# Gated linear attention and a mixture of experts: state read in four array tiles, another order of loads, filler matmuls

## The chip, the cores and the metric

One NeuronCore of a Trainium2 chip runs the whole kernel. The metric is device time in microseconds (us) for one execution: lower is better. The kernel before takes 489.4 us, the median of three runs (488.76 to 489.51). The profile is of one more execution, whose span from first to last instruction is 488.0 us.

## The reference, cut to what matters

Two layers follow one another. The first is a recurrent attention with a decay per channel. The second sends each row to the one expert that its gate prefers.

```python
# q, k, v, alpha: batch 4, heads 8, sequence 768, head size 48, float32
for t in range(S):
    state = alpha[:, :, t, :, None] * state + np.einsum('bhd,bhe->bhde', k[:, :, t], v[:, :, t])
    y[:, :, t] = np.einsum('bhd,bhde->bhe', q[:, :, t], state)
# x: the heads side by side, 3072 rows of 384
x = np.ascontiguousarray(y.transpose(0, 2, 1, 3)).reshape(B * S, H * D)
# experts: 8 of them, w1 384 x 1024, w2 1024 x 384
expert_idx = np.argmax(x @ w_gate, axis=1)
# for the rows of each expert e:
h = np.maximum(rows @ w1[e], 0.0)
out_rows = gate_weight * (h @ w2[e])
```

## The kernel before: the parts that matter here

The sequence is cut into 24 blocks of 128 rows, six to each batch entry. Within a block the recurrence becomes matrix products. Its running product of decays is the exponential of a running sum of logarithms. What earlier blocks left behind is a state `U`, read once per block. Heads go two by two: head `a` of a pair lies on partitions `64a` to `64a + 47`.

```python
def load(s, names):                      # 1024 runs of 192 bytes each
    for n in names:
        ...
        nc.sync.dma_start(t[:], src)
def cums(s):                             # running sum of ln(alpha), then two exponentials
    cum = ps.tile([C, Dm], F32, name="cum")
    nc.tensor.matmul(cum[:], lhsT=cmask[:], rhs=d["ln"][:], start=True, stop=True)
    ...
def attend(s):
    y = ps.tile([C, NP, C], F32, name="y")
    if c > 0:                            # the state read: NP = 4 pairs, two heads each
        for p in range(NP):
            for r in (0, DP):            # DP = 64
                nc.tensor.matmul(y[r : r + DP, p, :], lhsT=st[s - 1]["U"][r : r + D, p, :],
                                 rhs=d["qT"][r : r + D, p, :], start=(p == 0), stop=False, ...)
    for p in range(NP):                  # the block's own values
        for i, r in enumerate((0, DP)):
            nc.tensor.matmul(y[r : r + DP, p, :], lhsT=d["v"][:, 2 * p + i, :],
                             rhs=d["d" + "AB"[i]][:, p, :], start=(c == 0 and p == 0), stop=True, ...)
    kvp = ps.tile([C, NP * D + 4 * E], F32, name="kvp")   # what the block adds to the state, and ranks
    ...                                  # matmuls into kvp
    nc.vector.tensor_copy(d["yT"][:], y[:])
    ...                                  # the new U, on VectorE and GpSimd
```

`rows(s)` turns `yT` back into rows with the constant `back`, whose last columns also hold the gate's weights. `keep_rows(s)` stores them to DRAM (`x_rows`). `choose` picks the expert of each row, `rank_products` and `slots_of` work out its place among the expert's rows, `one_hots` and `tokens_of_slots` collect in one PSUM bank which token is in which place, and `indices` makes of it the list for the gathers.

```python
for s in range(-5, NT + 1):              # NT = 24
    do(load, s + 8 if s + 8 >= 4 else -1, "akq")
    do(load, s + 5, "v")
    do(logs, s + 5)
    do(cums, s + 4)
    do(operands, s + 3)
    do(transposes, s + 2)
    ...                                  # at s == NT: tokens of places, ranks, one-hots
    do(rows, s - 1)
    do(scores, s + 1)
    do(keep_rows, s - 1)
    ...
    do(attend, s)
    ...
    if s == 15:
        w_t[0] = fetch1(0), fetch2(0)    # all of expert 0's weights: two transfers
...
indices(range(NX, NX + NJ))              # three parts of one tile, g_idx
indices(range(NX))
indices(range(NX + NJ, PB))
```

The experts come in four pairs. Each pair gathers seven blocks of 128 rows, turns them, and goes through two layers. Nothing holds back the weights of experts 1 and 2: they are issued as soon as the queue gets to them.

```python
xg = gather(columns(0))
w_t[1] = fetch1(1), fetch2(1)
w_t[2] = fetch1(2), fetch2(2)
for p in range(EP):
    ...
    if p == 0:
        for j in range(2):
            turn(xg, j, ...)
        for f, hp in enumerate(begun):   # three tiles of hidden units on the first 256 rows
            products1(w_t[0][0], xTa, hp, f, 0, 2 * C)
        turn(xg, 2, ...)
        turn(xg, NH, ...)
    ha = layer1(...)
    for j in range(NH + 1, NJ):
        turn(xg, j, ...)
    ...
```

Of the kernel before, what the change touches and what calls it, by code (L numbers as in the profile page):

```python
# [18 lines left out]
def kernel(  # L19
# [10 lines left out]
):  # L30

# [42 lines left out]

    consts = ctx.enter_context(tc.tile_pool(name="consts", bufs=1))
# [7 lines left out]

    def first_consts():
        make_upper_triangular(nc, cmask[:], 1.0, diag=True)
        make_identity(nc, ident[:])
        for t in kqb:
            nc.vector.memset(t[:, :, :, D:], 0.0)
        for t in vb:
            nc.vector.memset(t[:, :, D:], 0.0)  # L90
        for t in Ub + Eb:
            nc.vector.memset(t[:], 0.0)

        for a in range(2):
            r = slice(a * DP, a * DP + D)
            nc.vector.tensor_copy(
                back[r, :, a * D : (a + 1) * D], ident[r, None, a * DP : a * DP + D].to_broadcast([D, NP, D]),
            )
            nc.vector.tensor_scalar_mul(back[r, :, D2:], back[r, :, D2:], -1.0)
# [57 lines left out]
    oh_c = rte.tile([C, NT, NC], F16)  # L157
    g_idx = rte.tile([C, NC], I32)
    tot = rte.tile([C, E], F32)

# [4 lines left out]
    def fetch1(ex):  # L165
        w1 = wpool.tile([C, DB, F], F32, name="w1")
        nc.sync.dma_start(w1[:], moe_w1[bass.ds(ex, 1)].rearrange("e (a p) f -> p (e a) f", p=C))
        return w1

# [4 lines left out]


    with tc.tile_pool(name="ld", bufs=6) as ld, \
         tc.tile_pool(name="work", bufs=2) as work, \
         tc.tile_pool(name="ps", bufs=1, space=PSUM) as ps, \
         tc.manual_schedule():
# [6 lines left out]
        def load(s, names):  # L186
            for n in names:
                src = rows_of({"a": alpha, "k": k, "q": q, "v": v}[n], s)
                if n == "v":
                    st[s][n] = vb[s % len(vb)]  # L190
                    nc.sync.dma_start(st[s][n][:, :, :D], src)
                else:
                    t = ld.tile([C, H, D], F32, name=n + "_sb", bufs=4 if n == "a" else 6)
                    nc.sync.dma_start(t[:], src)  # L194
                    st[s][n] = t
# [70 lines left out]
        def attend(s):  # L266
# [3 lines left out]
            y = ps.tile([C, NP, C], F32, name="y")  # L270
            if c > 0:
                for p in range(NP):
                    for r in (0, DP):
                        nc.tensor.matmul(  # L274
                            y[r : r + DP, p, :], lhsT=st[s - 1]["U"][r : r + D, p, :], rhs=d["qT"][r : r + D, p, :],
                            start=(p == 0), stop=False, skip_group_check=True,
                        )
            for p in range(NP):
                for i, r in enumerate((0, DP)):
                    nc.tensor.matmul(  # L280
                        y[r : r + DP, p, :], lhsT=d["v"][:, 2 * p + i, :], rhs=d["d" + "AB"[i]][:, p, :],
                        start=(c == 0 and p == 0), stop=True, skip_group_check=True,
                    )
            d["yT"] = work.tile([C, NP, C], F32, name="yT")
            kvp = ps.tile([C, NP * D + 4 * E], F32, name="kvp")
            kv = kvp[:, : NP * D].rearrange("r (p d) -> r p d", p=NP)
            ranked = [rank_products(g, kvp[:, NP * D : NP * D + len(g) * E]) for g in groups_of if g[-1] == s - 2]
            if c + 1 < NB:
                for p in range(NP):
                    for i, r in enumerate((0, DP)):  # L290
                        nc.tensor.matmul(  # L291
                            kv[r : r + DP, p, :], lhsT=kqb[s % 4][:, 0, 2 * p + i, :], rhs=d["v"][:, 2 * p + i, :D],
                            start=(p == 0), stop=True, skip_group_check=True,
                        )
            nc.vector.tensor_copy(d["yT"][:], y[:])  # L295
# [88 lines left out]
        def indices(blocks):  # L384
# [3 lines left out]
            gv = g_idx[:].rearrange("p (a b) -> p a b", a=EP)[:, :, blocks[0] : blocks[-1] + 1]  # L388
# [7 lines left out]

        nc.scalar.preload_act_table_set("natural_log_exp_and_others")
        for i in range(2):
            load(i, "akq")
        nc.gpsimd.memset(back[:], 0.0)  # L400
        for a in range(2):
            nc.scalar.dma_start(
                back[a * DP : a * DP + D, :, D2:], moe_w_gate.rearrange("(p a d) e -> a d p e", a=2, d=D)[a],
            )
        for i in range(2, 4):
            load(i, "akq")
        first_consts()
        hots = []
        for s in range(-5, NT + 1):
            do(load, s + 8 if s + 8 >= 4 else -1, "akq")  # L410
            do(load, s + 5, "v")
            do(logs, s + 5)
            do(cums, s + 4)
            do(operands, s + 3)
            do(transposes, s + 2)
            if s == NT:
                route = ps.tile([C, Dm], F32, name="cum")
                tokens_of_slots(0, 6)
                ranked = rank_products(groups_of[-2], ps.tile([C, NP * D + 4 * E], F32, name="kvp")[:, :E])
                while hots:  # L420
                    one_hots(hots.pop(0))
                slots_of(*ranked)
                one_hots(hots.pop(0))
# [8 lines left out]
            do(attend, s)  # L432
            for _ in range(2 if len(hots) > 2 else 1):
                if hots and s < NT:
                    one_hots(hots.pop(0))
            late_consts(s)
            if s == 15:
                w_t[0] = fetch1(0), fetch2(0)
        tokens_of_slots(6, NT - 1)
        slots_of(*rank_products(groups_of[-1], ps.tile([C, NP * D + 4 * E], F32, name="kvp")[:, :E]))  # L440
# [5 lines left out]
        indices(range(NX, NX + NJ))  # L446
        indices(range(NX))
        indices(range(NX + NJ, PB))
# [4 lines left out]
    xg_pool = ctx.enter_context(tc.tile_pool(name="moe_x", bufs=2))  # L453
# [41 lines left out]
    def gather(idx):  # L495

        xg = xg_pool.tile([C, len(idx), W], F32, name="xg")
# [70 lines left out]
    def columns(p):  # L568
        c0 = p * PB + NX
        return [g_idx[:, c0 + j : c0 + j + 1] for j in range(NJ)]  # L570
# [3 lines left out]
    with tc.manual_schedule():  # L574
        xg = gather(columns(0))
        w_t[1] = fetch1(1), fetch2(1)
        w_t[2] = fetch1(2), fetch2(2)
        for p in range(EP):
            idx = columns(p)
            a, b = 2 * p, 2 * p + 1  # L580
            xg_next = gather(columns(p + 1)) if p + 1 < EP else None
            if p == 0:

                xTa = wk.tile([C, DB, CAP], F32, name="xT", bufs=3)
                xTb = wk.tile([C, DB, CAP], F32, name="xT", bufs=3)
                for j in range(2):
                    turn(xg, j, (xTa, j * C, 0, C))
                begun = [hidden_tile() for _ in range(3)]
                for f, hp in enumerate(begun):
                    products1(w_t[0][0], xTa, hp, f, 0, 2 * C)  # L590
                turn(xg, 2, (xTa, 2 * C, 0, C))
                turn(xg, NH, (xTa, NH * C, 0, HB), (xTb, 0, HB, C))
            ha = layer1(w_t[a][0], xTa, CAP, begun, 2 * C)
            begun = ()
            for j in range(NH + 1, NJ):
                turn(xg, j, (xTb, HB + (j - NH - 1) * C, 0, C))
            gw = gates(xg, NJ)
            w1n = {e: fetch1(e) for e in (a + 3,) if e < E}
            for j in range(NH):
                layer2([(w_t[a][1], ha, j * C)], gw[:, j : j + 1], idx[j], True)  # L600
            hb = layer1(w_t[b][0], xTb, CAP)
            if b + 3 < E:
                w1n[b + 3] = fetch1(b + 3)
            if xg_next is not None:
                xTa = wk.tile([C, DB, CAP], F32, name="xT", bufs=3)
                xTc = wk.tile([C, DB, CAP], F32, name="xT", bufs=3)
                for j in range(NH):
                    turn(xg_next, j, (xTa, j * C, 0, C))
                turn(xg_next, NH, (xTa, NH * C, 0, HB), (xTc, 0, HB, C))
                xTb = xTc  # L610
            if p == 0:
                extra_blocks()
            layer2([(w_t[a][1], ha, NH * C), (w_t[b][1], hb, 0)], gw[:, NH : NH + 1], idx[NH], True)
            if a + 3 < E:
                w_t[a + 3] = w1n[a + 3], fetch2(a + 3)
            for j in range(NH + 1, NJ):
                layer2([(w_t[b][1], hb, HB + (j - NH - 1) * C)], gw[:, j : j + 1], idx[j], True)
            if b + 3 < E:
                w_t[b + 3] = w1n[b + 3], fetch2(b + 3)
# [44 lines left out]
```

## Time and profile before

| | before |
|---|---|
| median of three runs | 489.4 us |
| span of the profiled execution | 488.0 us |
| TensorE busy (matmul) | 457.6 us, 94% of the span |
| VectorE, ScalarE, GpSimd busy | 142.3, 103.2, 137.8 us |
| mean granted clock of TensorE | 0.979 |
| bytes moved by DMA | 59.76 MB, 127213 packets, 110304 of them under 512 bytes |

The page of a profile gives busy time per engine, then the span in 40 slices with a digit for each (9 is 90% or more busy). It goes on with transfers, the chain of work that ended last, and the costliest groups of instructions. A line such as `L274 PE MATMUL y<-qT,Ub` names the kernel's line, the engine, the operation, the tile written and the tiles read. A matmul on 32-bit floats leaves two records: the 160 matmuls of the state read (eight in each of 20 blocks) are 320 records; a transpose leaves one. The records of neighbouring matmuls overlap, so a busy TensorE is not one at its peak, and the distance from start to start tells the pace.

### The profile page before, as it was taken

Reading aid. Unit: us, or ns where it says so; the run is one execution under the profiler, and the core shown is the slowest. Engines: PE = TensorE matmul, PEld = TensorE weight load, DVE = VectorE, ACT = ScalarE, POOL = GpSimd, SP = SyncE. Lnnn points to the kernel's source line nnn. Section 1 sums busy time; section 2 is a strip of 40 time slices with the busy share of each in tenths; the row PEclk is TensorE's granted clock in tenths of the full one; section 3 lists DMA queues with packets and bytes.
Section 4 is the critical chain, followed back from the end, with each engine's and each line's share of the span. In section 5 each row is a group of like instructions: output and inputs, shape, how many; then the busy total and the mean of one; then the engine's idle time right before and its main releaser. Section 6 shows DMA issues by size and latency. Waiting matters only on the chain.

```text
span 488.0 us, 7370 instructions
## 1 busy us (share of the span) xinstructions
PE 457.6 (94%) x2881; PEld 297.4 (61%) x2881; DVE 142.3 (29%) x391; ACT 103.2 (21%) x209; POOL 137.8 (28%) x226
## 2 busy tenths in 40 slices
PE   2999999999999389999999999999999999999992
PEld 0788888888898275555555555555555455555451
DVE  2344766665778421212401201101201201301100
ACT  3544544544421001101001111011111001101010
POOL 3556745555642270010124010016020020010020
PEclk9999999999999779999999999999999999999997
DMA  9999999889992151300726400537300040000000
GB/s 161 199 177 203 207 210 203 168 170 272 299 356 107 50 160 39 142 32 8 267 75 211 135 32 0 189 118 249 129 28 16 1 166 22 1 20 16 2 32 25
DMA packets 127213, 59.76 MB, mean 122 GB/s; under 512 B 110304, under 2 KB 121604, under 8 KB 127178
## 3 DMA queue, kind: packets, MB, share of 16 engines
q1 hardware_dynamic: 114818, 48.87, 39.6%
q0 software_dynamic: 3584, 10.34, 6.4%
q10 hardware_dynamic: 8776, 0.08, 1.0%
q8 instruction: 23, 0.38, 0.3%
q14 instruction: 12, 0.10, 0.1%
HBM read 49.70 MB, written 10.35 MB: 123 GB/s over the span
## 4 chain that ended last, share of the span: by engine, by line
issue 54%; PE 27%; POOL 11%; DVE 2%; DMA 2%; SPq 1%; ACT 0%; POOLq 0%; ACTq 0%
POOL out_dram L559 6%; POOL xg L499 5%; PE sA L254 5%; PE y L280 4%; PE tp L241 4%; PE xr L313 4%; PE cum L210 4%; PE y L274 4%; PE kvp L291 2%; SPq L194 1%; DMA a_sb<-in_alpha_dram 1%; DMA x_rows<-xs 1%; DVE yT L295 1%; DVE sc L330 0%; DVE dA L258 0%
## 5 line engine op out<-in xcount | busy, mean ns | idle before, releaser
L528 PE MATMUL hp<-xT,w 128*128 128x448 f32 (+2 forms) x402 | 148.4, 530 | 1.2 <-DVE xT L524 1.2
L553 PE MATMUL zp<-w,h_sb 128*128 128x384 f32 (+1 forms) x512 | 146.8, 488 | 0.0
L528 PEld LDWEIGHTS hp<-xT,w 128*128 128x128 f32 x402 | 77.4, 194 | 69.9 <-issue 65.0
L553 PEld LDWEIGHTS zp<-w,h_sb 128*128 128x128 f32 (+1 forms) x512 | 81.1, 177 | 62.4 <-issue 13.6
L559 POOL DMA_INDIRECT out_dram<-zo,g_idx x28 | 27.7, 988 | 251.7 <-ACT zo L558 251.7
L542 DVE TENSOR_SCALAR h_sb<-hp 128x448 f32<-128x448 f32 x32 | 20.0, 624 | 218.4 <-PE hp L528 218.4
L544 ACT ACTIVATE h_sb<-hp 128x448 f32<-128x448 f32 x32 | 17.4, 543 | 142.0 <-PE hp L528 142.0
L558 ACT ACTIVATE zo<-zp,gw 128x384 f32<-128x384 f32 x28 | 16.3, 581 | 133.6 <-PE zp L553 129.0
L210 PE MATMUL cum<-ln,cmask 128*128 128x384 f32 x48 | 24.7, 601 | 8.7 <-ACT cp L214 4.4
L499 POOL DMA_INDIRECT xg<-x_rows,g_idx x28 | 26.9, 960 | 12.2 <-issue 12.2
L241 PEld LDWEIGHTS tp<-ident,kqb 128*128 128x128 f32 x192 | 23.5, 146 | 7.9 <-issue 4.2
L254 PE MATMUL sA<-qT,kT 48*128 48x128 f32 x192 | 27.7, 285 | 0.0
L254 PE MATMUL sB<-qT,kT 48*128 48x128 f32 x192 | 27.7, 285 | 0.0
L233 POOL TENSOR_TENSOR kqb<-k_sb,icp 128x384 f32<-128x384 f32 x24 | 23.9, 996 | 8.8 <-ACT icp L213 8.6
L241 PE MATMUL tp<-ident,kqb 128*128 128x128 f32 x192 | 26.2, 282 | 0.0
L280 PE MATMUL y<-dA,vb 128*64 128x128 f32 x192 | 26.1, 279 | 0.0
L280 PE MATMUL y<-dB,vb 128*64 128x128 f32 x192 | 26.1, 279 | 0.0
L313 PE MATMUL xr<-back,yT 128*128 128x104 f32 x192 | 25.4, 275 | 0.7 <-DVE yT L295 0.5
L261 POOL TENSOR_SCALAR_AFFINE_SELECT dB<-dB 128x512 f32<-128x512 f32 x24 | 15.2, 634 | 37.3 <-ACT dB L260 23.8
L254 PEld LDWEIGHTS sA<-qT,kT 48*128 48x128 f32 x192 | 23.1, 187 | 2.6 <-issue 0.3
L313 PEld LDWEIGHTS xr<-back,yT 128*128 128x128 f32 x192 | 23.3, 192 | 1.5 <-issue 1.0
L234 POOL TENSOR_TENSOR kqb<-q_sb,cp 128x384 f32<-128x384 f32 x24 | 23.9, 996 | 0.0
(117 smaller groups left out, 403.0 us busy)
## 6 DMA issues: line engine op xcount, KB each, us to landing
w<-in_moe_w_dram SPq DMA_DIRECT2D x16, 1536.0 KB, 6.8
x_rows<-xs SPq DMA_DIRECT2D x24, 196.0 KB, 2.9
a_sb<-in_alpha_dram SPq DMA_DIRECT2D x24, 192.0 KB, 4.1
k_sb<-in_k_dram SPq DMA_DIRECT2D x24, 192.0 KB, 3.8
q_sb<-in_q_dram SPq DMA_DIRECT2D x24, 192.0 KB, 4.0
vb<-in_v_dram SPq DMA_DIRECT2D x24, 192.0 KB, 4.6
Eb<-decay_rows ACTq DMA_DIRECT2D x40, 0.8 KB, 3.0
xg<-x_rows,g_idx POOLq DMA_INDIRECT x28, 3.1
```

The source lines that it names most:

```text
L210: nc.tensor.matmul(cum[:], lhsT=cmask[:], rhs=d["ln"][:], start=True, stop=True)
L233: nc.gpsimd.tensor_tensor(kq[:, 0, :, :D], d["k"][:], heads(d["icp"]), op=ALU.mult)
L234: nc.gpsimd.tensor_tensor(kq[:, 1, :, :D], d["q"][:], heads(d["cp"]), op=ALU.mult)
L241: nc.tensor.transpose(tp[:, p, :], pair(kqb[s % 4][:, i], p), ident[:])
L254: nc.tensor.matmul(t[:, p, :], lhsT=d["kT"][r : r + D, p, :], rhs=d["qT"][r : r + D, p, :], start=True, stop=True,)
L280: nc.tensor.matmul(y[r : r + DP, p, :], lhsT=d["v"][:, 2 * p + i, :], rhs=d["d" + "AB"[i]][:, p, :], start=(c == 0 and p == 0), stop=True, ...
L313: nc.tensor.matmul(xr[:, p, :], lhsT=d["yT"][:, p, :], rhs=back[:, p, :], start=True, stop=True)
L499: nc.gpsimd.indirect_dma_start(out=xg[:, j, :], out_offset=None, in_=x_d[:, :], in_offset=bass.IndirectOffsetOnAxis(ap=i, axis=0),)
L528: nc.tensor.matmul(hp[:, c0:c1], lhsT=w1[:, a, f * C : (f + 1) * C], rhs=xT[:, a, c0:c1], start=(a == 0), stop=(a == DB - 1), skip_group_c ...
L542: nc.vector.tensor_relu(h[:, f, :cols], hp[:, :cols])
L553: nc.tensor.matmul(zp[i * m : (i + 1) * m, :], lhsT=h[:, f, c0 : c0 + m], rhs=w2[:, f, :], start=(f == 0), stop=(f == FB - 1), skip_group_ ...
L559: ins = nc.gpsimd.indirect_dma_start(out=out[:, :], out_offset=bass.IndirectOffsetOnAxis(ap=idx, axis=0), in_=zo[:], in_offset=None, bound ...
```

## The change

It has four aims.

- **The state read in four tiles.** The pairs 0 and 1 write as before. The pairs 2 and 3 write into a second bank, the one that also holds `kvp`, and with their two heads' results swapped between the halves of the partitions. So four matmuls in a row use the four quarters of the array. The swap is undone in `back`, whose rows for these pairs are swapped too. The copy of `y` becomes two copies.
- **Loads in order of need.** Each block's loads of v, k, q and alpha are issued by how soon they are used. Up to block 0 a block's attention comes ahead of the later block's running sum. Expert 0's weights come in 20 small transfers; those of experts 1 and 2 wait until the first rows have been turned.
- **The array kept busy.** Matmuls on a tile of zeros, whose results nobody reads, are put in where the array would stand idle at the start and at the end of the attention[...].
- **A shorter end of the attention.** The first gathers' indices get a tile of their own, made first, and the last block's choice comes ahead of the one-hots of the block before.

The diff, cut:

```diff
+    def at(p, a):
+        return DP * (a ^ (p >= NP // 2))
 ...
-            y = ps.tile([C, NP, C], F32, name="y")
+            y = ps.tile([C, NP // 2, C], F32, name="y")
+            kvp = ps.tile([C, 2 * C + NP * D + 4 * E], F32, name="kvp")
+            y2 = kvp[:, : 2 * C].rearrange("r (p t) -> r p t", p=NP // 2)
 ...
+                for n in range(NP // 2):
+                    for p in (n, n + NP // 2):
+                        for a in range(2):
+                            r = a * DP
+                            nc.tensor.matmul(
+                                yp(p)[at(p, a) : at(p, a) + DP, :],
+                                lhsT=st[s - 1]["U"][r : r + D, p, :], rhs=d["qT"][r : r + D, p, :],
+                                start=(n == 0), stop=False, skip_group_check=True,
+                            )
 ...
-            nc.vector.tensor_copy(d["yT"][:], y[:])
+            nc.vector.tensor_copy(d["yT"][:, : NP // 2, :], y[:])
+            nc.vector.tensor_copy(d["yT"][:, NP // 2 :, :], y2)
 ...
+        AHEAD = 4
+        def loads(s):
+            for n, i in (("v", s + AHEAD), ("k", s + 3 + AHEAD), ("q", s + 3 + AHEAD), ("a", s + 4 + AHEAD)):
+                if 0 <= i < NT:
+                    load(n, i)
 ...
+        def keep_busy(n):
+            if n:
+                t = ps.tile([C, NP, D2 + E], F32, name="xr")[:].rearrange("r p t -> r (p t)")
+            for _ in range(n):
+                nc.tensor.matmul(
+                    t[:, : 2 * C], lhsT=still[:, :C], rhs=still[:], start=True, stop=True, skip_group_check=True,
+                )
 ...
+        keep_busy(4)
+        parts = fetch_parts(0)
-        for s in range(-5, NT + 1):
+        for s in range(-5, NT):
+            loads(s)
             do(logs, s + 5)
-            do(cums, s + 4)
-            do(operands, s + 3)
+            if s > 0:
+                do(cums, s + 4)
+                do(operands, s + 3)
             do(transposes, s + 2)
+            if s == -2:
+                keep_busy(2)
 ...
             do(attend, s)
+            if s <= 0:
+                do(cums, s + 4)
+                if s < 0:
+                    do(operands, s + 4)
+                else:
+                    back_consts()
+                keep_busy({-4: 4, -3: 3, -2: 1}.get(s, 0))
 ...
+            if s >= 8:
+                next(parts, None)
+                if s >= NT - 6:
+                    next(parts, None)
 ...
+        rows(NT - 1)
+        keep_rows(NT - 1)
+        choose(groups_of[-1])
+        one_hots(hots.pop(0))
+        tokens_of_slots(7, NT - 1)
+        slots_of(*rank_products(groups_of[-1], ps.tile([C, NP, C], F32, name="sB")[:, 0, :E]))
+        keep_busy(3)
         one_hots(NT - 1)
         tokens_of_slots(NT - 1, NT)
 ...
+        keep_busy(5)
+        indices(g_mid, range(NX, NX + NJ))
+        indices(g_idx, range(PB))
 ...
             for f, hp in enumerate(begun):
+                if f == 2:
+                    turn(xg, 2, (xTa, 2 * C, 0, C))
+                    turn(xg, NH, (xTa, NH * C, 0, HB), (xTb, 0, HB, C))
                 products1(w_t[0][0], xTa, hp, f, 0, 2 * C)
 ...
         for j in range(NH + 1, NJ):
             turn(xg, j, ...)
+        if p == 0:
+            for e in (1, 2):
+                w_t[e] = fetch1(e, True), fetch2(e)   # True: a write by VectorE into w1 comes first
```

## The prediction

> **What bounds the kernel now.** I read the page's head first, for which engine is full and when.
>
> ```profile
> PE 457.6 (94%) x2881; PEld 297.4 (61%) x2881; DVE 142.3 (29%) x391; ACT 103.2 (21%) x209; POOL 137.8 (28%) x226
> ...
> PE   2999999999999389999999999999999999999992
> ...
> PEclk9999999999999779999999999999999999999997
> DMA  9999999889992151300726400537300040000000
> ```
>
> A slice is 12.2 us. TensorE is full from about 12 us to the end but for one hole in slices 13 and 14 (159 to 183 us), where the granted clock also falls to 0.7. The hole parts the attention (up to about 158 us) from the experts. The DMA engines are full in the attention alone. So three places matter to this change: the attention's step, its start, and the hole.
>
> The step. In the timeline, filtered to TensorE, one full step reads (scores, L254, and values, L280, are left out because they come matmul by matmul):
>
> ```profile
> 117.96 1.09 PE L274 MATMUL y<-qT,Ub 48*64 48x128 f32 x16
> 119.90 0.62 PE L291 MATMUL kvp<-vb,kqb 128*64 128x48 f32 x16
> 120.45 0.91 PE L210 MATMUL cum<-ln,cmask 128*128 128x384 f32 x2
> 121.20 1.04 PE L241 MATMUL tp<-ident,kqb 128*128 128x128 f32 x8
> 122.08 1.04 PE L313 MATMUL xr<-back,yT 128*128 128x104 f32 x8
> 124.13 1.09 PE L274 MATMUL y<-qT,Ub 48*64 48x128 f32 x16
> ```
>
> The columns are start, length, engine, line, operation and count. From state read (L274) to state read is 124.13 - 117.96 = 6.17 us, and each group starts where the one before stops. The waits view, cut to 22 to 157 us, lists a single wait of TensorE, 0.5 us. So there whatever is taken off TensorE comes off the time, until another engine or a transfer fills. The next fullest, VectorE, is busy 86.4 of those 135 us.
>
> The start is different: the logarithm of each block of alpha waits for its load.
>
> ```profile
> 13.77 0.53 ACT L199 ACTIVATE ln<-a_sb 128x384 f32<-128x384 f32 x1 [1.84 <-DMA a_sb<-in_alpha_dram]
> 17.48 0.52 ACT L199 ACTIVATE ln<-a_sb 128x384 f32<-128x384 f32 x1 [1.96 <-DMA a_sb<-in_alpha_dram]
> 21.26 0.52 ACT L199 ACTIVATE ln<-a_sb 128x384 f32<-128x384 f32 x1 [1.54 <-DMA a_sb<-in_alpha_dram]
> ```
>
> These are alpha of blocks 3, 4 and 5, the 10th, 14th and 18th load: about 0.94 us per load once v is among them. From 17.85 us on the timeline shows TensorE without a gap.
>
> The hole, in the timeline:
>
> ```profile
> 164.13 0.21 PE L443 MATMUL cum<-ohs,ones_sq 128*128 128x8 f16 x1
> 164.41 0.19 DVE L390 TENSOR_SCALAR up<-cum 128x28 f32<-128x28 f32 x1 [0.45 <-PE cum L443]
> ...
> 165.43 0.24 DVE L391 SCALAR_TENSOR_TENSOR g_idx<-cum,up 128x84 int32<-128x84 f32 x1
> ...
> 166.67 1.21 POOL L499 DMA_INDIRECT xg<-x_rows,g_idx  x1 [3.96 <-issue]
> ...
> 170.25 1.84 PE L522 MATMUL xtp<-ident,xg 128*128 128x128 f32 x6 [5.91 <-DMA xg<-x_rows,g_idx]
> ...
> 172.74 6.56 PE L528 MATMUL hp<-xT,w 128*128 128x256 f32 x18 [0.65 <-DVE xT L524]
> ```
>
> The last routing matmul ends at 164.34, and TensorE waits 5.91 us for the first gathered rows. What follows is slow as well: the view by stretches has the clock at
>
> ```profile
> 166.00:169.00 3.00, 0.00 (x0) 0.00 (x0) 0.00 (x0) 0.00 (x0) 2.03 (x2) 0.50 0.16 31
> 169.00:172.00 3.00, 1.69 (x6) 1.01 (x6) 0.56 (x1) 0.00 (x0) 2.09 (x4) 0.50 0.57 168
> ...
> 175.00:178.00 3.00, 3.00 (x9) 2.40 (x8) 0.00 (x0) 0.00 (x0) 2.27 (x3) 0.56 0.57 151
> 178.00:180.00 2.00, 1.95 (x12) 1.51 (x11) 0.34 (x1) 0.00 (x0) 1.51 (x2) 1.00 0.56 166
> ```
>
> where the third number from the end is the clock: half speed from some 164 to 177.5 us, though TensorE works again from 170 on.
>
> **What the Trainium skill says.** (1) "TensorEngine Tiling (Array Packing)", Tiling Modes: with 64 rows and 64 columns the array holds four tiles that run in parallel. The trace before uses only two of them in the state read (48x64 stationary): sixteen records in 1.02 us, where the two column tiles of L280 also take 0.92 (21.75 to 22.67). It can't show whether four overlap. (2) The same page, Gotcha 1: different row tiles must not write one PSUM bank at the same time. This is why the change sends two pairs to a second bank. No run shows the contrary. (3) "TensorE: Matmul & The Clock Gate", Back-to-back issue gap: a floor of some 25 ns from matmul start to start. The closest thing here is L291, sixteen records in 0.55 us, 34 ns each. (4) The same page, "What's actually happening": the clock halves after an idle window of about 3.4 us and comes back after a busy one. The trace agrees: the clock falls near 164 after three thin microseconds, and returns at 177.5 some 7 us after work resumed.
>
> **Part by part.**
>
> *State read.* Eight matmuls are sixteen records. Two tiles give 107 ns per pair of records (L280's starts in the timeline are 0.11 us apart), so 8 x 0.107 = 0.86, and 1.02 with the change of shape ahead of it: 0.16. With four tiles, perfectly: 4 x 0.107 + 0.16 = 0.59. If the records come no closer than L291's 34 ns: 16 x 0.034 + 0.16 = 0.70. The saving is 0.32 to 0.43 us a step. I take 0.36. Twenty of 24 blocks read a state: 20 x 0.36 = 7.2. The last two or three steps have no running sum or transposes and VectorE fills there (4.48 of 5 us from 152 to 157), so I count 18: **6.5 us**. Beside it: the copy of y becomes two, one more VectorE instruction of about 0.1 us a step. Rows wait for yT a step later (1.5 us of slack at 102 to 103.5), and the new state is ready 2 us before its use, so neither should show.
>
> *Order at the start.* The order of the alpha loads is as before: alpha of block 5 is still the 18th. What moves is the array's order: block 0 is now attended before the running sum of block 4, and block 5's sum is the first that waits for its load, which is ready at 21.26 + 0.5 = 21.8. The work TensorE has done by then is what it had done at 23.22 before (the sum of block 5 in the timeline). Gain 23.2 - 21.8 = **1.4 us**. From there loads come every 4 us or so per step and TensorE needs over 5. Keeping the array warm shortens its first sums (1.65 against 0.75 us), but these wait for loads anyway.
>
> *End of the attention.* Indices for the first gathers now take one pair of operations: 165.67 - 164.85 = 0.8 saved. One pair of one-hots leaves the chain ahead of the last block's choice (0.5). The last rows' store (issued at 162.01, 2.9 us to land by the page's median) would then end last, so I count **1.0 us** of the 1.3.
>
> *Clock in the hole.* A record of 256 columns takes 2 x 0.107 = 0.213 us at full clock by L280's rate, so the 18 of L528 above would take 3.84 us, and took 6.4 cold. Five added matmuls of two records each take 5 x 0.427 = 2.1 us. The idle stretch shrinks from 5.9 to about 5 - 2.1 = 3 us, less than a window. Warm, layer 1 would save 6.4 - 3.8 = 2.6, the transposes up to 0.6, and the turning of rows between the second and third group of products hides a wait of 0.6: 3.8 in all. A window that catches most of the idle time could still halve the clock for one window, and cost 1.7. Weighing this at about even, **3.0 us**. The three fillers behind the last ranks (1.28 us) lie in a wait of 1.43 us (162.58 to 164.01).
>
> *Weights.* Those of expert 0 come in 20 pieces from block 8 on; those of experts 1 and 2 only after the first layer 1. They start near 196 us and 1.5 MB takes some 5 to 7 us, while expert 1 is first needed about 212 (196.4 plus three second layers of 5.1 us). No gain, no loss.
>
> Sum: 6.5 + 1.4 + 1.0 + 3.0 = 11.9 us; 489.4 - 11.9 = 477.5.
>
> **Rivals.** *Four tiles do not overlap.* Then the state read stays at 1.02 and there is 5.4 us of gain, 484. For it: the trace never shows more than two tiles at once. Against it: row pairs (L254) and column pairs (L280) both overlap already, and nothing else in the array differs. *DMA becomes the bound.* A step loads four blocks of 0.197 MB and stores 0.2 MB: 0.99 MB, at the 216 GB/s seen between 70 and 80 us is 4.6 us, 5.3 with a piece of weights. TensorE would need 5.8. Close, but the loads run ahead; a loss of 0.3 us in some steps would cost 2 to 4 us, 480. *The fillers cost.* If the clock has already fallen, three fillers take 2.6 us instead of 1.3 and hold the last routing matmul up by 1.1; with the clock falling all the same the end brings nothing: about 481. *Late weights* of expert 1 would show as a wait of several us before its first layer; the 8 us of margin speaks against it.
>
> **Range and chances.** The parts run from 4 to 9 (state), 0 to 3 (start), 0 to 1.5 (end) and 1 to 4 (clock). Extremes don't come together: 470 to 484. The 2% line is 479.6, 2 us above the middle, so faster by over 2% gets 0.7, within 2% 0.27, slower 0.03.
>
> **What would show it.** State reads of sixteen records in 0.6 to 0.7 us, and 5.8 us from one to the next; the running sum of block 5 near 21.8; the first gather about 1 us sooner after the last attend; the clock near 1.0 between 170 and 178 on the old scale; no wait of TensorE on weights. It is wrong if the state read still takes 1 us, if new waits of TensorE on yT, kvp or loads appear inside the steps, or if the clock falls as before.

## The result and the profile after

| | before | after |
|---|---|---|
| median of four runs | 489.1 us (488.7 to 489.5) | 477.0 us (476.2 to 477.8) |
| span of the profiled execution | 488.0 us | 475.9 us |
| TensorE busy | 457.6 us | 454.8 us |
| mean granted clock | 0.979 | 0.990 |

The ratio of the times is 0.9753, with a 95% interval of 0.9733 to 0.9772. The prediction said 477.5 us, and 11.9 us of gain; it is 12.1. The sum fits better than its terms do, as the rest of this text shows.

The slices of the changed kernel's page, of 11.9 us each:

```profile
PE   8799999999998799999999999999999999999992
...
PEclk9999999999999899999999999999999999999997
```

The first slice is 8 instead of 2: those are mainly the fillers. The hole between the attention and the experts is 8 and 7 where it was 3 and 8, and the clock falls to 8 in one slice where it was 7 in two. TensorE is busy 2.8 us less, though it now also runs the fillers.

One full step in the timeline of TensorE (start, length, line, operation and count), cut to the state read, the first value product behind it and the next state read:

```profile
100.23 0.33 PE L329 MATMUL y<-qT,Ub 48*64 48x128 f32 x2
100.24 0.33 PE L329 MATMUL kvp<-qT,Ub 48*64 48x128 f32 x2
...
100.83 0.32 PE L336 MATMUL y<-dA,vb 128*64 128x128 f32 x1
...
105.98 0.33 PE L329 MATMUL y<-qT,Ub 48*64 48x128 f32 x2
```

In the kernel before, a state read and the first value product behind it:

```profile
105.60 1.09 PE L274 MATMUL y<-qT,Ub 48*64 48x128 f32 x16
106.62 0.32 PE L280 MATMUL y<-dA,vb 128*64 128x128 f32 x1
```

The state read takes 100.83 - 100.23 = 0.60 us instead of 106.62 - 105.60 = 1.02, and the step 5.75 us instead of 6.17. The first records for `y` and for the second bank in `kvp` start 0.01 us apart. The groups between have their old lengths.

The start, in the timeline of ScalarE and TensorE (ACT is ScalarE; brackets hold the idle time before and what ended it):

```profile
17.01 0.52 ACT L244 ACTIVATE ln<-a_sb 128x384 f32<-128x384 f32 x1 [2.10 <-DMA a_sb<-in_alpha_dram]
...
17.44 0.57 ACT L291 COPY kT<-tp 128x512 f32<-128x512 f32 x1
...
18.15 0.63 PE L286 MATMUL tp<-ident,kqb 128*128 128x128 f32 x4 [0.87 <-ACT kT L291]
...
20.89 0.52 ACT L244 ACTIVATE ln<-a_sb 128x384 f32<-128x384 f32 x1 [1.62 <-DMA a_sb<-in_alpha_dram]
21.28 0.91 PE L255 MATMUL cum<-ln,cmask 128*128 128x384 f32 x2
...
22.67 0.48 ACT L259 ACTIVATE cp<-cum 128x384 f32<-128x384 f32 x1
23.21 0.91 PE L255 MATMUL cum<-ln,cmask 128*128 128x384 f32 x2 [1.02 <-ACT cp L259]
```

The logarithm of block 5 (20.89) came as expected. Block 5's running sum is the second of the two sums shown, at 23.21, and it doesn't wait for that logarithm: it waits for the last exponential of block 4 (L259), which reads the same PSUM tile `cum`. Block 4's own sum (21.28) was late: it now comes behind block 0's attention, and TensorE waited there, at 18.15, for a copy (`kT`) that stands in ScalarE's queue behind the logarithm of block 4 (17.01). Before the change block 5's sum was no later:

```profile
23.22 0.91 PE L210 MATMUL cum<-ln,cmask 128*128 128x384 f32 x2
```

The hole, in the timeline:

```profile
155.42 0.17 PE L528 MATMUL cum<-ohs,ones_sq 128*128 128x8 f16 x1
155.45 2.40 PE L460 MATMUL xr<-still 128*128 128x256 f32 x10
...
156.36 1.21 POOL L584 DMA_INDIRECT xg<-x_rows,g_mid  x1 [2.86 <-DVE up L448]
...
159.79 0.52 PE L607 MATMUL xtp<-ident,xg 128*128 128x128 f32 x3 [1.94 <-DMA xg<-x_rows,g_mid]
...
162.21 4.54 PE L613 MATMUL hp<-xT,w 128*128 128x256 f32 x12 [0.65 <-DVE xT L609]
```

The first gather starts 0.94 us after the last routing matmul, where it took 2.54, and TensorE waits 1.94 us for rows where it waited 5.91; part of that wait is now filled with matmuls on zeros (L460). From the routing to the first turned rows it is 4.37 us instead of 6.12. The stretches of the same trace (busy times with counts, then clock, DMA share and GB/s) have the clock lost here:

```profile
162.00:165.00 3.00, 2.79 (x7) 2.25 (x8) 0.15 (x1) 0.00 (x0) 2.39 (x3) 0.55 0.65 161
```

In the stretch ahead of it the clock is 1.00, in the one behind it 0.88: some 3.4 us at half speed, where it was about 13.7 before.

The value products of the last block start, before the change, at

```profile
156.61 0.32 PE L280 MATMUL y<-dA,vb 128*64 128x128 f32 x1
```

and in the changed kernel at

```profile
147.87 0.32 PE L336 MATMUL y<-dA,vb 128*64 128x128 f32 x1
```

With these and other marks, the two timelines of TensorE say where the 12.1 us of span came off:

| mark | before | after | saved so far |
|---|---|---|---|
| running sum of block 5 starts | 23.22 | 23.21 | 0.0 |
| value products of the last block start | 156.61 | 147.87 | 8.7 |
| last routing matmul | 164.13 | 155.42 | 8.7 |
| first rows turned | 170.25 | 159.79 | 10.5 |
| third group of turns, after the first layer | 194.84 | 182.74 | 12.1 |

From the last mark on both kernels take equally long.

### The profile page after: what moved, and what is told of

It reads as the page before. It is cut to its first block, busy times and chain, and to the rows that moved or that the text cites. A ratio compares the mean times of both kernels' runs of the same rounds, so it can differ in the third digit from the quotient of the medians.

```text
span 475.9 us, 7519 instructions
## 1 busy us (share of the span) xinstructions
PE 454.8 (96%) x2925; PEld 295.2 (62%) x2925; DVE 146.0 (31%) x420; ACT 103.7 (22%) x209; POOL 138.1 (29%) x226
## 4 chain that ended last, share of the span: by engine, by line
issue 54%; PE 26%; POOL 10%; DVE 3%; SPq 2%; DMA 2%; POOLq 0%; ACT 0%; ACTq 0%
POOL out_dram L644 6%; PE sA L299 5%; PE xr L371 4%; POOL xg L584 4%; PE tp L286 4%; PE cum L255 3%; PE y L336 2%; SPq L235 2%; PE y L329 2%; PE kvp L336 2%; PE kvp L348 2%; DMA a_sb<-in_alpha_dram 2%; PE hp L613 1%; DMA xg<-x_rows,g_mid 1%; DVE oh_c L430 0%
## 5 line engine op out<-in xcount | busy, mean ns | idle before, releaser
L644 POOL DMA_INDIRECT out_dram<-zo,g_mid x28 | 27.7, 988 | 249.9 <-ACT zo L643 232.7
L584 POOL DMA_INDIRECT xg<-x_rows,g_mid x28 | 26.9, 960 | 11.1 <-issue 7.6
L286 PEld LDWEIGHTS tp<-ident,kqb 128*128 128x128 f32 x192 | 22.2, 141 | 8.7 <-issue 5.8
L286 PE MATMUL tp<-ident,kqb 128*128 128x128 f32 x192 | 25.2, 273 | 1.6 <-ACT kT L291 0.9
L255 PE MATMUL cum<-ln,cmask 128*128 128x384 f32 x48 | 21.9, 537 | 1.4 <-ACT cp L259 1.4
L299 PEld LDWEIGHTS sB<-qT,kT 48*128 48x128 f32 x192 | 23.1, 187 | 0.0
L289 DVE COPY qT<-tp 128x512 f32<-128x512 f32 x24 | 16.5, 687 | 19.4 <-PE tp L286 19.4
(135 smaller groups left out, 454.8 us busy)
```

The costliest lines, as they stand in the source:

```text
L286: nc.tensor.transpose(tp[:, p, :], pair(kqb[s % 4][:, i], p), ident[:])
L299: nc.tensor.matmul(t[:, p, :], lhsT=d["kT"][r : r + D, p, :], rhs=d["qT"][r : r + D, p, :], start=True, stop=True,)
L584: nc.gpsimd.indirect_dma_start(out=xg[:, j, :], out_offset=None, in_=x_d[:, :], in_offset=bass.IndirectOffsetOnAxis(ap=i, axis=0),)
L644: ins = nc.gpsimd.indirect_dma_start(out=out[:, :], out_offset=bass.IndirectOffsetOnAxis(ap=idx, axis=0), in_=zo[:], in_offset=None, bound ...
```

## The experiments

My theory after this result: the four tiles overlap, and that gives 20 x 0.42 = 8.4 us; the indices give 1.7 us and the hole's clock and order 1.6; the start gives nothing, as ScalarE's queue holds it. The rivals: the second bank or the order of issue and not the quarters makes the read fast; the attention's gain comes from the loads and not from the read; the fillers do nothing. In the four runs `no_swap`, `four_near`, `logs_late` and `no_start_fill` the chip was another one, on which the kernel before took 492.4 us (488.9 to 489.3 on the chips of the other runs); every ratio is against the kernel before on the same chip.

### Order of issue: two_tiles

The changed kernel with the pairs in plain order, so that the four matmuls for `y` are issued ahead of the four for `kvp`:

```diff
-for n in range(NP // 2):
-    for p in (n, n + NP // 2):
+for p in range(NP):
-    ... start=(n == 0)
+    ... start=(p % (NP // 2) == 0)
```

> The changed kernel with the state read issued pair after pair (0, 1, 2, 3) again, so that neighbouring matmuls share two quarters of the array; second bank, swap and everything else stay. Theory (four quarters at once give the gain, and only if the four matmuls stand side by side): each of 20 state reads goes back from 0.60 to about 1.0 us, the step from 5.75 to 6.15, and the time to 477 + 20 x 0.4 = 485 us (484 to 486). Rival (the second bank alone gives it, as two pairs no longer share one): the state read stays at 0.60 and the time at 477.

Measured: 477.83 us, ratio 0.9773 (0.9756 to 0.9789). The timeline of TensorE:

```profile
99.55 0.33 PE L328 MATMUL y<-qT,Ub 48*64 48x128 f32 x2
99.58 0.33 PE L328 MATMUL kvp<-qT,Ub 48*64 48x128 f32 x2
99.71 0.28 PE L328 MATMUL y<-qT,Ub 48*64 48x128 f32 x2
```

The starts alternate between `y` and `kvp`, though the program has all matmuls of `y` first. The read is as short as in the changed kernel. My expectation that the alternating order is needed fell: matmuls for quarters that are free start ahead of earlier ones whose quarters are not.

### Quarters or bank: no_swap

The changed kernel with the second bank kept and the swap taken out, in the matmuls and in `back` alike:

```diff
-        return DP * (a ^ (p >= NP // 2))
+        return DP * a
```

> The changed kernel without the swap: pairs 2 and 3 still write into the second bank, but each head's result stays in its own half of the partitions, so only two quarters of the array are used; the constants follow. Theory (the swap, that is the third and fourth quarter, gives the gain; the order of issue does not matter): state read back at 1.02 us, step 6.17, time 477 + 20 x 0.42 = 485.4 us (484 to 486.5). Rival (the second bank is what lets the matmuls overlap): state read 0.60 and 477 us.

Measured: 491.41 us, ratio 0.9976 (0.9955 to 0.9997). The timeline of TensorE:

```profile
104.34 0.44 PE L329 MATMUL y<-qT,Ub 48*64 48x128 f32 x4
104.61 0.38 PE L329 MATMUL kvp<-qT,Ub 48*64 48x128 f32 x4
...
110.52 0.44 PE L329 MATMUL y<-qT,Ub 48*64 48x128 f32 x4
```

Now the banks take turns, four records every 0.22 to 0.32 us up to the end of the read, and the step is 110.52 - 104.34 = 6.18 us, where it was 6.17 before the change. The last value products start at 155.28, 7.4 us later than in the changed kernel. A second bank alone buys nothing; the third and fourth quarter do. Whether they need the second bank is untested: no run has the swap in one bank. That the total gained so little is partly something else: TensorE waits 4.4 us once at the first hidden units there, as it does (2.7 to 4.4 us) in all four kernels of that chip and not in the changed kernel's trace. Why is open; the kernel before is 3.3 us slower on that chip as well.

### The read alone: four_only, four_near

The kernel before with nothing but the new state read (matmuls, copies of `y`, `back`); all loads, orders and ends as before:

> The kernel before with the four-tile state read alone: second bank, swap, swapped constants and two copies of y, but the old loads, order and end, and no fillers. Theory (the state read is 20 x 0.42 = 8.4 us of the gain and does not need the rest): 489.1 - 8.4 = 480.7 us (479.5 to 482). Rival (loads or the two copies hold the shorter step back without the new order): 483 or more, with new waits of TensorE in the steps.

Measured: 486.87 us, ratio 0.9931 (0.9908 to 0.9954): 2.4 us of gain, where I had expected some 8. The state read was 0.6 us here too, but the last value products start at 153.79, only 2.8 us sooner than before. The timeline of SyncE's queue, ScalarE and TensorE shows the loss (SPq is the queue that issues loads and stores):

```profile
38.90 0.81 SPq L339 DMA_DIRECT2D x_rows<-xs  x1
...
44.47 0.48 ACT L337 COPY xs<-xr 128x384 f32<-128x384 f32 x1 [5.41 <-DMA x_rows<-xs]
45.00 2.04 PE L330 MATMUL xr<-back,yT 128*128 128x104 f32 x8 [2.81 <-ACT xs L337]
```

A row block is copied into a buffer that must first have been stored. The first store is issued at 38.90, behind 37 loads in the one queue. TensorE waits 2.81 us, its next group takes 2.04 us instead of 1.04, and the clock falls to 0.5. So the faster array ran into the loads that run ahead. If that is the cause, fewer loads ahead of the store must free it:

```diff
-            do(load, s + 8 if s + 8 >= 4 else -1, "akq")
-            do(load, s + 5, "v")
+            do(load, s + 7 if s + 7 >= 4 else -1, "akq")
+            do(load, s + 4, "v")
```

> The kernel with the four-tile state read alone (486.9 us), with one more edit: loads run seven blocks ahead instead of eight (v four instead of five), so that four fewer loads stand in the queue ahead of the first store of rows. Theory (that store, issued at 38.9 us behind 37 loads of about 1 us, was what held the array for 5 us at 42 to 49 us): the first store is issued near 35 us, no wait of TensorE on the copy of rows, 481 us (480 to 482). Rival (the queue was not at fault; transfers are simply too slow for the shorter step): 485 to 487 us with the wait elsewhere.

Measured: 484.63 us, ratio 0.9844 (0.9787 to 0.9901). The store and the last block's first value product in its timeline:

```profile
34.90 1.04 SPq L339 DMA_DIRECT2D x_rows<-xs  x1
...
147.65 0.32 PE L295 MATMUL y<-dA,vb 128*64 128x128 f32 x1
```

It is issued 4 us sooner, behind 33 loads. TensorE has no wait from 22 to 60 us, and the last value products start at 147.65, as in the changed kernel (147.87). The changed kernel's own first store is issued at 34.52, behind 34 loads. The 481 us I expected were for the first chip; the ratio makes 481.4 of its 489.1, though with an interval of 478.7 to 484.2. So, by the timeline, the read gives the whole gain of the attention, but only if the queue is shallow enough; the change's order of loads, which looks like housekeeping, lets it show. Fewer loads ahead with the old read were not run; `no_swap`, which has the changed kernel's loads and the old read, reaches its last value products only 1.3 us sooner than the kernel before.

### The fillers at the end: no_end_fill, more_fill, after_again

The changed kernel without the fillers of the end, `keep_busy(3)` and `keep_busy(5)`:

> The changed kernel without the eight fillers at the end of the attention. Theory (the fillers shorten the cold time from some 13 to some 4 us of clock at half): the clock falls near 155 and comes back only some 7 us after work resumes; layer 1 of the first pair ends 1.5 to 3 us later, 478.5 to 480 us. Rival (the gain there is the order of turns and the shorter chain, and the fillers do nothing, as the clock fell with them too): 477 us within 0.5, layer 1 as long after the first rows as with them.

Measured: 477.56 us, ratio 0.9764 (0.9744 to 0.9783). The stretch:

```profile
162.00:165.00 3.00, 3.00 (x8) 2.38 (x8) 0.00 (x0) 0.00 (x0) 2.39 (x3) 0.50 0.61 154
```

The clock is at half from 156 to about 166 us. But the 478.5 to 480 us of my theory did not come: by its time this kernel can't be told from the changed one. The routing is where it was, 7.5 us after the last value products, so the three early fillers cost nothing. Next, more of them: eight instead of five behind the routing, and three between the turned rows and the first products.

```diff
-        keep_busy(5)
+        keep_busy(8)
 ...
+            begun = [hidden_tile() for _ in range(3)]
             for j in range(2):
                 turn(xg, j, (xTa, j * C, 0, C))
-            begun = [hidden_tile() for _ in range(3)]
+                for n in ((192, 192), (256,))[j]:
+                    nc.tensor.matmul(begun[2][:, :n], lhsT=still[:, :C], rhs=still[:, :n], start=True, stop=True, ...)
```

> The changed kernel with eight fillers of 256 columns instead of five behind the routing, and three more (192, 192 and 256 columns) between the first turned rows and the first products. Theory (what is left of the cold time, about 3.3 us at half clock from 162 to 165.4, comes from the idle stretch 157.9 to 162.2): the clock stays at 1.0 throughout and layer 1 ends 1.5 us sooner, 475.4 us (474.8 to 476.2). Rival (fillers do not count, or they delay the first turned rows as much as they warm): 477 or more.

Measured: 475.42 us, ratio 0.9717 (0.9701 to 0.9733). The stretch:

```profile
162.00:165.00 3.00, 3.00 (x19) 2.67 (x18) 0.17 (x1) 0.00 (x0) 2.16 (x3) 1.00 0.57 155
```

The clock stays full, and 19 records fit where the kernel without fillers has 8. From the first turned rows to the third group of turns it now takes 21.3 us; it was 24.6 before, 23.0 in the changed kernel and 23.8 without fillers. Last, the changed kernel once more, unedited:

> The changed kernel once more, as the measure for the other three runs on this chip. Both theories: 0.975 of the kernel before if the chip is as the first, 0.98 to 0.985 if it is as the second, where the runs without swap, with late logarithms and without starting fillers were taken.

Measured: 476.39 us (474.88 to 478.06), ratio 0.9751 (0.9714 to 0.9788). This time its clock held:

```profile
162.00:165.00 3.00, 3.00 (x19) 2.67 (x18) 0.66 (x2) 0.00 (x0) 2.39 (x3) 1.00 0.58 152
```

and the same stage took 21.2 us. The same program thus falls on either side, 1.8 us apart in this stage. "TensorE: Matmul & The Clock Gate" in the Trainium skill ("What's actually happening") says that the window of activity runs freely and that the outcome varies from run to run for that reason; the two traces (0.55 and 1.00 in one stretch) agree. Over all runs it is the same: the mean clock of the changed kernel's eight runs was 0.987 to 0.990 in five and 0.996 in three, while the eight runs of `more_fill` and `best_start` (below) had 0.993 or more. Without the fillers 24.6 - 23.8 = 0.8 us of the stage's gain remain, which I put down to the order of turns (it was not undone by itself); the fillers bring another 0.8 when the clock is lost all the same, 2.6 when it holds.

### The start: logs_late, no_start_fill, best_start

For the first turns the logarithm of the later block is put behind the exponentials of the earlier one in ScalarE's queue:

```diff
-            do(logs, s + 5)
+            if s > 1:
+                do(logs, s + 5)
 ...                                  # after attend, cums and fillers
+            if s <= 1:
+                do(logs, s + 5)
```

> The changed kernel with the logarithm of each block at the end of its turn, instead of the beginning, for the turns up to block 1, so that in ScalarE's queue it no longer stands, waiting for its load, ahead of the copies and exponentials of earlier blocks. Theory (this order held up block 0's attention and the running sum of block 5): that sum starts near 21.6 us, 0.7 to 1.6 sooner than in the runs with the changed kernel's order, time 476 us (475.2 to 476.6). Rival (loads alone pace the start, and ScalarE's order follows them): 477 us and the sum at 22.2 to 23.2.

Measured: 485.19 us, ratio 0.9851 (0.9805 to 0.9897). Timeline of ScalarE and TensorE:

```profile
21.38 0.49 ACT L258 ACTIVATE icp<-cum 128x384 f32<-128x384 f32 x1 [2.75 <-DMA Eb<-decay_rows]
...
22.71 1.65 PE L255 MATMUL cum<-ln,cmask 128*128 128x384 f32 x2 [3.28 <-ACT ln L244]
```

Half right. The sum of block 4 came sooner (18.52 instead of 21.28), but then ScalarE stood 2.75 us behind the issue of a transfer that reads the decay row back, and block 5's sum came only 0.5 us sooner. TensorE had been idle 3.28 us by then, and the stretch that follows shows the price:

```profile
25.00:30.00 5.00, 5.00 (x47) 4.52 (x48) 1.48 (x3) 1.39 (x4) 0.00 (x0) 0.62 1.11 220
```

With the clock near 0.6 through the next step, block 6's sum came at 31.37, where the changed kernel has it at 28.96. The changed kernel without any filler before and in the first turns:

```diff
-        keep_busy(4)
-            if s == -2:
-                keep_busy(2)
-                keep_busy({-4: 4, -3: 3, -2: 1}.get(s, 0))
```

> The changed kernel without the fillers at the start. Theory (loads and ScalarE's order pace the start, so a cold array costs nothing): running sum of block 5 no later than with them, 22.2 to 23.2 us, time 477 us within 0.6. Rival (a cold array lengthens the chain from load to operands): the sum 0.5 to 1.5 us later, 477.5 to 478.5 us.

Measured: 484.29 us, ratio 0.983 (0.9783 to 0.9878). Block 5's sum is no later (22.79), but TensorE has waited 1.77 us for block 4's exponential (1.02 in the changed kernel), the clock is 0.82 in the stretch from 20 to 25 us, and block 6's sum starts at 30.20, 1.2 us later than in the changed kernel and 2.2 later than in its repetition. That the missing fillers did this is not shown: the last of them starts at 12.8 us in the changed kernel, and here the clock was full (1.00) from 15 to 20 us without them. In both runs, though, an array idle ahead of block 5's sum (3.28 and 1.77 us) is followed by a lower clock. From both: put the exponentials first, then the logarithm, and the transfers of the decay row last in ScalarE's queue, with four fillers for the time of waiting, and add the fillers of `more_fill`:

```diff
-            do(decay_out, s + 3)
-            do(decay_in, s + 2)
+            if s > 1:
+                do(decay_out, s + 3)
+                do(decay_in, s + 2)
 ...
-                keep_busy({-4: 4, -3: 3, -2: 1}.get(s, 0))
+                keep_busy({-4: 4, -3: 3, -2: 1, 0: 4}.get(s, 0))
+            if s <= 1:
+                do(logs, s + 5)
+                do(decay_out, s + 3)
+                do(decay_in, s + 2)
```

> The changed kernel with the additional end fillers (475.4 us), and up to block 1 with ScalarE's queue reordered: exponentials of the running sum first, then the next block's logarithm, then the two transfers of the decay, which in the run with late logarithms had become the wait instead; four fillers stand in the wait for block 5's load. Theory (loads set the start once ScalarE's order does not, and the array must not be left idle there): block 5's running sum at 21.3 to 21.8 us, array at full clock, 0.7 to 1.5 us under the run with the end fillers: 474 to 474.8 us, or 2.2 to 3 us under the changed kernel on the same chip. Rival (something else in the first 22 us sets it): no sooner than 22.2 us and 475.4.

Measured: 474.27 us (474.0 to 474.62), ratio 0.9699 (0.968 to 0.9718), below every run of the changed kernel beside it. The timeline:

```profile
19.28 1.89 PE L460 MATMUL xr<-still 128*128 128x256 f32 x8
...
20.29 0.53 ACT L244 ACTIVATE ln<-a_sb 128x384 f32<-128x384 f32 x1
21.00 0.81 PE L255 MATMUL cum<-ln,cmask 128*128 128x384 f32 x2
```

Block 5's sum starts at 21.00, right behind its logarithm. That is what my prediction took the change to do by itself, at 21.8. The order and the four fillers were not tried one without the other. Against `more_fill` (22.55) it is 1.55 us sooner, and the last routing matmul 1.64 sooner.

### The first gather and the weights: pool_late, w_now

The change also reserves the memory of the first gathered rows early. With it reserved after the attention's buffers, as before:

```diff
-    xg_pools = [ctx.enter_context(tc.tile_pool(name="moe_x0", bufs=1))]
+    xg_pools = []
 ...
+    xg_pools.append(ctx.enter_context(tc.tile_pool(name="moe_x0", bufs=1)))
     xg_pools.append(ctx.enter_context(tc.tile_pool(name="moe_x1", bufs=1)))
```

> The changed kernel with the memory of the first gathered rows set aside after the attention's buffers are given back, as before, instead of ahead of them. Theory (of the 1.75 us by which the first gather starts sooner after the routing, 0.85 are the two pairs of index operations, the rest the release of the attention's buffers, for which the gather had to wait): the first gather starts 0.8 to 1.0 us later after the last routing matmul, time 0.8 to 1 us more. Rival (all of it is the index order): gather as soon, same time within 0.4.

Measured: 478.76 us (478.2 to 479.37), ratio 0.9785 (0.9764 to 0.9806). In its timeline the last routing matmul starts at 156.10 and the first gather at 157.05, 0.95 us later, as in the changed kernel (0.94). The memory makes no difference there, so it doesn't account for the quicker gather; the indices of their own remain, which were not undone by themselves. The kernel is 2.4 us slower than the changed one beside it all the same. In the profiled run 1.7 us of this is there by the last routing matmul (156.10 against 154.43), most of it already in block 5's sum (23.89 against 22.21), and the clock was lost in the hole. Why all its runs are slower I can't say.

The weights of experts 1 and 2 no longer held back, but issued right behind the first gather:

```diff
     xg = gather(columns(0))
+    for e in (1, 2):
+        w_t[e] = fetch1(e), fetch2(e)
 ...
-        if p == 0:
-            for e in (1, 2):
-                w_t[e] = fetch1(e, True), fetch2(e)
```

> The changed kernel without holding back the weights of experts 1 and 2: they are issued right behind the last store of rows. Theory (6.3 MB at some 300 GB/s then run beside the first gathers and slow them): rows gathered 1 to 4 us later, a wait of the array on gathers of 3 us or more ahead of layer 1, 1 to 4 us more in all. Rival (as predicted: no gain and no loss): same time within 0.5 us.

Measured: 480.74 us, ratio 0.9841 (0.9815 to 0.9866), 4.3 us slower than the changed kernel beside it. The stretch behind the attention:

```profile
159.00:162.00 3.00, 0.87 (x3) 0.50 (x3) 0.00 (x0) 0.00 (x0) 2.39 (x3) 0.50 1.05 383
```

The transfers run at 383 GB/s beside the gathers (145 in the changed kernel), rows take 7.0 us from the routing to the array instead of 4.3, and the wait costs the clock too. Before the change these weights were issued during the attention, from 125.9 to 137.6 us. Holding them back brings nothing by itself; it avoids a loss once they are no longer loaded there.

## Why the prediction was nearly right

*State read: expected 6.5 us, measured 8.7 by the last value products.* The mechanism was right: four quarters work at once, and `no_swap` shows that the swap is what gives them. The saving of one read was too small: sixteen records take 0.60 us, 0.42 saved and not 0.36. I had taken the middle between perfect overlap and the 34 ns pace of L291's kind, and it is perfect: four records in 0.11 us. The count of 18 was nearly right. Step by step, 15 reads gave 0.42 each, 6.3 us; the last two steps, where VectorE fills, only 0.27 and 0.13; and three steps that had been longer before (6.33, 6.39 and 6.52 us) also came down to 5.75, 2.0 us together. Why those three were longer isn't shown. The reason given for the second bank does not hold as it stands. "No run shows the contrary" of the rule that different row tiles must not write one bank at the same time was wrong: the two records at 100.23 above belong to the two heads of a pair, which lie in different row halves of the array, and both write `y`, on different partitions; so they did before. What no run shows is two row halves writing the same partitions of one bank.

*Order at the start: expected 1.4 us, measured 0.0 in this trace.* This step failed: "block 5's sum is the first that waits for its load, which is ready at 21.26 + 0.5 = 21.8". The load and the logarithm came on time, at 20.89. But I had overlooked two other waits. First, all blocks' sums are written to one tile, `cum`, so block 5's sum must wait until block 4's exponentials have read it: in all eight traces with this order it starts 1.93 to 2.25 us behind block 4's sum. Second, block 4's sum now comes behind block 0's attention, and that waits for ScalarE, where a copy stands behind a logarithm that waits for its load. So block 4's sum moved from 18.94 to 21.28, and block 5's stayed at 23.21; with that logarithm put later (`logs_late`) block 4's sum came at 18.52. In seven other runs with this order and its fillers block 5's sum started at 21.8 to 23.9: in six 0.5 to 1.4 us ahead of the 23.22 before, in one 0.7 behind. `best_start` got there at 21.0 by changing ScalarE's order and filling the wait. "These wait for loads anyway" is true of the first sums, but an idle array there is not free: in `logs_late` the step after it took 2.9 us longer.

*End of the attention: expected 1.0 us, measured 1.75.* The indices' part, 0.8, was too small: the first gather starts 1.6 us sooner after the routing. It starts 0.3 us behind its own indices, where it started 1.0 us behind the last of three parts; what took that time before is not shown. But up to the last routing matmul nothing was gained: it comes 7.55 us after the last value products, and came 7.52 before. The order of choices and one-hots, which I had counted at 0.5, brought nothing. The last rows' store did not become the bound.

*Clock in the hole: expected 3.0 us, measured 1.6.* "Weighing this at about even" was the right form: the profiled run of the changed kernel lost the clock for a while, the repeated one did not, and there the same stage was 24.6 - 21.2 = 3.4 us shorter than before. The difference, 1.8 us, is about the 1.7 that the prediction gave one window of half clock.

*Weights.* As predicted, there is no wait on them. `w_now` shows that the order matters, in the other direction.

*The rivals.* "Four tiles do not overlap" is refuted. "DMA becomes the bound" I had thought of as a rate, 0.3 us in some steps. `four_only` shows it as an order in a queue: the read alone gave 2.4 us. I did not see that the load order belongs to the state read's gain. "The fillers cost" is refuted: the routing takes 7.54 us with and without the three.

So that the sum, 11.9, came out so close is luck: terms too small by 2.2 and 0.75 stood beside terms too large by 1.4 and 1.4.

## What to carry to other kernels

Small matmuls that use half of the array can be brought to four quarters by swapping where half of the results go, if a later product with a constant can undo the swap; the quarters give the gain, not a second bank alone and not the order of issue. After each such shortening look at what else is issued in order, both the queue in which a store stands behind loads that run ahead and the queues of the other engines, because the array's next wait is there. Fill a wait of 2 to 4 us ahead of dense matmuls with matmuls on zeros, and generously: with the change's own number the clock was left to chance, with six more it held.

## What the runs showed of the hardware

- Matmuls start out of program order when their quarter of the array is free (`two_tiles`: `y` and `kvp` alternate 0.03 us apart, though the four of `y` stand first in the program). "TensorE: Matmul & The Clock Gate" in the Trainium skill (Part 3, The mechanism) says that starts keep program order strictly; here the trace differs, and decides.
- Two matmuls in different row halves of the array write one PSUM bank at the same time, on different partitions: two records in `y` at 100.23 in the changed kernel.
- Matmuls on a tile of zeros keep the clock up: `more_fill` had 1.00 where the kernel without fillers had 0.50.
- An idle 3.3 us at the start cost almost as much again in the step after it (`logs_late`): block 6's sum was 2.4 us later than in the changed kernel though block 5's was 0.5 us sooner, 2.9 us lost in one step at a clock of about 0.6.
- A transfer that waits for its data in ScalarE's queue holds that engine's computation: 2.75 us in `logs_late`.
- A store behind loads is late by their issue: three or four loads fewer ahead of it, and it is issued 4 us sooner (38.90 against 34.90 and 34.52).
